# Attention and a low-rank mixer on one core: the first batch's v loaded in two halves, separate places for its heads' probabilities, and the second group's copies on two engines

## The chip, the core and the metric

The kernel runs on one core of one Trainium2 chip. The metric is the device time in microseconds of one execution. The kernel before was run three times (383.29, 383.66 and 385.33 us; the median, 383.66 us, is its time). One more execution was profiled, and every duration in the text comes from that one.

## The reference

Two layers follow each other. The first is causal attention with a bias made of running sums; the second is a low-rank mixer over the sequence and a feed-forward network (FFN) with a ReLU.

```python
B, H, S, D = 8, 8, 576, 64
scores = (q @ k.T) / sqrt(D)                      # per batch and head
cum = cumsum(max(s, 0), axis=-1)
bias = -(cum[:, :, :, None] - cum[:, :, None, :])
scores = where(causal, -1e9, scores + min(bias, 0))
attn = softmax(scores)                            # sum + 1e-9
x = (attn @ v) -> [B, S, H * D = 512]
h = x.T @ U @ V                                   # U: [576, 32], V: [32, 576]
u = x + h.T
out = u + max(u @ w_ch1, 0) @ w_ch2               # w_ch1: [512, 2048], w_ch2: [2048, 512]
```

Inputs and output are float32. The kernel computes in bfloat16 with float32 accumulation.

## The kernel before, in words

**Groups.** The eight batches form five groups: (0,), (1,), (2, 3), (4, 5), (6, 7). A group goes through two parts. The *front* (`front`) is its attention and its mixing (`attention`, then `mix`); the *back* (`ffn`) is its FFN. The front of group g + 1 is woven into the back of group g, so that TensorE always has FFN products between the small steps of the attention. Group 0 has no back to hide in: its front is `first_attention`, which runs by itself at the start.

**The order is the program's.** The kernel is scheduled by hand (`manual_schedule`): each engine executes its instructions in the order in which the Python code emits them, and semaphores are added for the data. `attention`, `mix` and `ffn` are generators that yield the cost, in microseconds, of what they have just emitted. The loop at the end (lines 829 to 847) emits a piece of the back, adds its cost times a ratio to an account `due`, and emits pieces of the front as long as the account is positive:

```python
ratio = FRONT[g + 1] / (BACK[g] - LEAD[g] - LAG[g])
due, live = -LEAD[g] * ratio, True
```

`FRONT` and `BACK` are the summed costs. `LEAD[g]` is how much of the back of group g is emitted before the next front begins; `LAG[g]` is how much is meant to be left when that front has ended.

**How q and k get into place.** TensorE needs q and k with the head dimension on the partitions. For the first two groups, `load_six` loads them by a DMA issued on GpSimd (which also converts to bfloat16) into tiles `six` of 96 partitions, two heads or four at a time, and `turn_six` turns a pair of heads: six TensorE transposes (line 438) into one PSUM bank, then two copies (line 451) out of it, one from partitions 0 to 63 and one from 64 to 127, into the even and odd columns of `kT` or `qT`. Its argument `by` names the engines of the two copies; without it both are on VectorE. For later groups, q and k go through DRAM (`kq_rows`) and DMA transposes on SyncE (`turn_kq`).

**Attention of a head.** `scores` makes the scores of one head in four quanta (lines 459 and 466). Each fills one of three PSUM banks `ps_s`, and ScalarE takes the exponential (line 471) into a tile `p` of probabilities. For the first group masked entries are made very negative by extra products (`bound`, line 466); for later groups VectorE masks `p` (line 631). `weigh` multiplies a head's `p` with v (15 products, line 511, into one of two banks `ps_pv`) and VectorE divides by the row sums (lines 517, 521, 526). The tiles `p` come from a ring of five, `pT`. The last two rows of tiles are read with their ends padded, so `clear` sets the columns behind `P_END` to zero once at the start.

**The first batch.** `first_attention` turns the first two pairs of heads, calls `prepare_second` (which emits GpSimd's loads for the second group and w2), and then goes over the eight heads. Between a head's quanta it places a `stir` (products without use, which keep TensorE active), a turn of a later pair, a `weigh` of an earlier head, or a step of the second group's running sums (`cumulate(1, 2)`). The last pair's k (`turns[6]`) is turned after head 3, its q (`turns[7]`) after head 4. After the loop come the mixing of the first batch (`ux_first`, `turn_first`) and the first three blocks of its FFN (`begin`, line 587).

**GpSimd's queue.** Before the heads GpSimd issues, in this order: k and q of heads 0 to 1, 2 to 3, 4 to 5 (`load_six`, line 203); all of the first batch's v (`load_v(0)`: four transfers of 128 rows, line 229, and a tail of 64 rows, line 235); k and q of heads 6 to 7; the four pieces of w1 (line 247). `prepare_second` continues with U and V, k and q of batch 1, v of batch 1 and the four pieces of w2 (line 253). A transfer issued on GpSimd first waits until the one eight issues before it has landed, because there are eight semaphores for them. SyncE issues the smaller transfers: rows of the running sums, the rows of ones, U, V, s, and the stores.

**Space.** Until the first FFN fills it, the tile `hT` (seen as `flat`, 18432 columns) holds other things: U and V and the rows of ones (`ones`, columns 2048 to 2623), the first batch's `six` (4096 to 10239) and the source of `stir` (10240 to 10367). The FFN's block nf writes columns 1152 nf to 1152 nf + 511 of it at first (line 786).

Of the kernel before, what the change touches and what calls it, by code (L numbers as in the profile page):

```python
# [24 lines left out]
TAIL = 4  # L25
# [6 lines left out]
P_W = P_END + 64  # L32
AUG = 4

A_K, A_Q, A_ONE, A_ALL = slice(0, 4), slice(3, 7), slice(3, 6), 7
# [12 lines left out]
def kernel(  # L48
# [12 lines left out]
    nc = tc.nc  # L61
    B, H, S, D = q.shape
# [6 lines left out]
    BH = B * H  # L69
# [31 lines left out]
    pT = [const([128, P_W], BF16, f"pT{i}") for i in range(5)]  # L101
# [20 lines left out]
    aug = nc.dram_tensor("aug_rows", (A_ALL, BH, S), BF16, kind="Internal").ap()  # L122
# [13 lines left out]
    flat = hT[:, :, :].rearrange("p a c -> p (a c)")  # L136
    stage = flat[:, :2048].bitcast(FP32)
    stirrer = flat[:, 10240:10368]
    ones = flat[:BH, 2048 : 2048 + S]
    n6 = H * SUB * D  # L140
    later = [const([128, H, SUB * D], BF16, f"six{i}") for i in range(2)]
    six = [
# [25 lines left out]
    def load_UV():  # L168
        nc.sync.dma_start(
            out=U_f[:, :4], in_=moe_U[:512].rearrange("(t p) r -> p t r", p=128)  # L170
        )
        nc.sync.dma_start(out=U_f[:64, 4], in_=moe_U[512:576])
        nc.sync.dma_start(out=V_f[:R], in_=moe_V)
        nc.sync.dma_start(out=U_f[64:128, 4], in_=moe_U[512:576])
        nc.sync.dma_start(out=V_f[R : 2 * R], in_=moe_V)
# [24 lines left out]
    def load_six(g, h0, h1):  # L200
        hs = slice(h0, h1)
        for to, src in zip(six[g], (k, q)):
            nc.gpsimd.dma_start(  # L203
                out=to[:, hs, :].rearrange("p h (s d) -> p h s d", d=D),
                in_=src[GROUPS[g][0], hs].rearrange("h (p s) d -> p h s d", s=SUB),
            )
# [15 lines left out]
                    transpose=True,  # L222
                )

    def load_v(g):
        dest = v_raw[g % 2]
        for bi, b in zip(SIDES[g], GROUPS[g]):
            for t in range(4):
                nc.gpsimd.dma_start(  # L229
                    out=dest[:, 5 * bi + t, :, :D],  # L230
                    in_=v[b, :, 128 * t : 128 * t + 128].rearrange("h p d -> p h d"),
                )
        for bi, b in zip(SIDES[g], GROUPS[g]):
            c = 64 * (bi or g == 0)
            nc.gpsimd.dma_start(
                out=dest[c : c + 64, TAIL, :, :D],
                in_=v[b, :, 512:576].rearrange("h p d -> p h d"),
            )

    def load_group(g):  # L240
# [130 lines left out]
    for t in (U_cat, V_cat):  # L371
# [5 lines left out]
        out=before_v, in_=before_v, compare_op=ALU.is_ge, fill=0.0, base=0,  # L377
# [3 lines left out]
        out=before_v, in_=before_v, compare_op=ALU.is_ge, fill=0.0, base=-1,  # L381
# [4 lines left out]
    for _ in cumulate(0, 1):  # L386
# [3 lines left out]
        out=neg[:, 64:], in_=neg[:, 64:], compare_op=ALU.is_ge, fill=NEG, base=0,  # L390
        pattern=[[1, 128]], channel_multiplier=-1,
    )
    for base, c, m in ((64, 1, -1), (-64, 0, 1)):
        nc.gpsimd.affine_select(
            out=neg[:, :64], in_=neg[:, :64], compare_op=ALU.is_ge, fill=NEG, base=base,
            pattern=[[c, 64]], channel_multiplier=m,
        )
    load_v(0)
    load_six(0, 6, 8)
    load_UV()  # L400
    load_s(1, B)
    place_ones(SECOND, (nc.sync, nc.sync))
    for j in range(4):
        load_w1(j)
    nc.sync.dma_start(
        out=aug[A_ONE].rearrange("r n s -> n r s"),
        in_=ones.unsqueeze(1).to_broadcast([BH, 3, S]),
    )
    for t in pT:
        clear(t[:, P_END:])  # L410
    nc.sync.dma_start(
        out=kq[:, :, PAIR:].rearrange("i n c -> (i n) c"), in_=pT[0][: 2 * BH // 2, P_END:]
# [119 lines left out]
    def next_p():  # L532
        n_p[0] += 1
        return pT[(n_p[0] - 1) % len(pT)]

    def first_attention():

        turns = [(hp, which) for hp in range(4) for which in range(2)]
        for i, (hp, which) in enumerate(turns[:4]):
            if i == 1:
                turn_six(0, hp, which, (nc.scalar.copy, nc.scalar.copy))
            else:
                turn_six(0, hp, which)
            stir((3, 14, 6, 46)[i])
        prepare_second()
        done, second = [], cumulate(1, 2)
        for h in range(H):  # L550
            n, hh = h // 2, h % 2
            p = next_p()
            quanta = scores(kT_all, qT_all, p, PW * n + S * hh, 448, True)
            next(quanta)
            next(quanta)
            if h == 7:
                ux_first((0, 1), nc.vector.tensor_copy)

            if h > 4:
                weigh(*done.pop(0))  # L560
            else:
                stir(3)
            next(quanta)
            if h < 4:
                stir(4)
            next(quanta)
            done.append((0, p, 0, h))
            if h in (2, 4, 6):
                next(second)
            if h < 2:  # L570
                turn_six(0, *turns[h + 4])
            elif h == 3:
                turn_six(0, *turns[6])
            elif h == 4:
                turn_six(0, *turns[7], (nc.scalar.copy, nc.vector.tensor_copy))
            if h > 3:
                weigh(*done.pop(0))
        turn_first((0, 1), 0, 256, nc.scalar.copy)
        ux_first((2,), nc.vector.tensor_copy)
        weigh(*done.pop(0))  # L580
        turn_first((0, 1), 256, 512, nc.scalar.copy)
        turn_first((2,), 0, 512, nc.scalar.copy)
        begun = [bank("s", 3) for _ in range(3)]

        def begin(nf, kts, c0, c1):
            for kt in kts:
                nc.tensor.matmul(
                    begun[nf][:, c0:c1], lhsT=w1[:, kt, 128 * nf : 128 * nf + 128],
                    rhs=uT[:, kt, c0:c1], start=(kt == 0 and c0 == 0), stop=False,
                )  # L590

        for nf in range(3):
            begin(nf, (0, 1), 0, 256)
        ux_first((3,), nc.vector.tensor_copy)
        for nf in range(3):
            begin(nf, (0, 1), 256, 512)
        for nf in range(3):
            begin(nf, (2,), 0, 512)
        turn_first((3,), 0, 256, nc.vector.tensor_copy)
        turn_first((3,), 256, 512, nc.scalar.copy)  # L600
        for _ in second:
            pass
        return begun
# [7 lines left out]
    def attention(g, side):  # L611

        pending = None
        turns = [(hp, which) for hp in range(4) for which in range(2)] if g == 1 else []


        for cost in (0.25, 1.8, 0.9) if turns else ():
            turn_six(g, *turns.pop(0))
            yield cost
        for hp in range(H // 2):  # L620
            n = pairs.index((g, hp))
            for hh in range(2):
                for i, bi in enumerate(SIDES[g]):
                    p = next_p()
                    quanta = scores(
                        kT_all, qT_all, p, place(n).start + (2 * i + hh) * S,
                        512 if bi == 0 else 448,
                    )
                    yield next(quanta)
                    yield next(quanta)  # L630
                    nc.vector.tensor_tensor(  # L631
                        p[:, D4:O1], p[:, D4:O1], keep[bi], ALU.min
                    )
                    if turns:
                        turn_six(g, *turns.pop(0))
                        yield 0.25
                    if pending is not None:
                        weigh(*pending)
                        yield 0.48
                    for cost in quanta:  # L640
                        yield cost
                    pending = (g, p, bi, 2 * hp + hh)
                    for _ in range(2):
                        next(side, None)
                    if n > 10 and (hh, i) == (0, 0):
                        bias_rows(n + 1)
            if g == 1 and hp == 1:
                nc.vector.tensor_copy(x_sb[1][:64, TAIL, :], x_sb[0][:64, TAIL, :])


            late = {5: 8, 6: 9, 7: 10, 8: 11}
            if n - 1 in late:
                bias_rows(late[n - 1])
            if n in late:
                turn_kq(late[n])
            if n > 9:
                turn_kq(n + 2)
            if g == 2 and hp == 0:

                for t in (kT(11), qT(11)):  # L660
                    nc.gpsimd.tensor_copy(hold, t[:1, PW : PW + 1])
                load_group(g + 1)
            if g > 2 and hp == 1:

                c = (2 * hp) * D
                nc.gpsimd.tensor_copy(hold, x_sb[g % 2][:1, 0, c : c + 1])  # L666
                load_group(g + 1)
        weigh(*pending)
        yield 0.48
        for _ in side:  # L670
            pass
# [147 lines left out]

    LEAD = [5.0, 11.0, 8.0, 0.0]
    FRONT = [0.0, 17.3, 24.6, 22.3, 22.3]
    BACK = [27.4, 34.3, 61.7, 61.7, 61.7]

    LAG = [0.0, 0.0, 4.5, 4.5]

    begun = first_attention()
    for g in range(len(GROUPS)):
# [48 lines left out]
```

## Time and profile before

| what | value |
|---|---|
| median of three runs | 383.66 us |
| the profiled execution: its time, and the span from its first to its last instruction | 384.49 us, 382.8 us |
| busy share of the span: TensorE, ScalarE, VectorE, GpSimd | 96%, 54%, 42%, 17% |
| mean granted TensorE clock | 0.991 |
| first product of group 0's FFN on the full inner dimension (line 606) | 35.82 us |
| first product with w2 (line 791) | 51.42 us |
| group 1's first FFN product | 84.80 us |
| group 2's first FFN product | 146.84 us |

The names of the engines in the profile are PE (TensorE's products), PEld (its weight loads), ACT (ScalarE), DVE (VectorE), POOL (GpSimd) and SP (SyncE). A line of the timeline gives the start in us, the busy time, the engine, the line of the kernel, the operation, what is written from what, the count, and in brackets how long the engine stood idle before it and what released it. Instructions of one kind that follow each other are merged into one line. A matmul's own duration counts its way through the array, so that consecutive ones overlap.

### The profile page before, as it was taken

To read this page: it belongs to the slowest core of one execution; us is meant where nothing else is said; L and a number is where in the kernel's file an instruction comes from. 1 tells how busy PE (TensorE), PEld (TensorE's weight loads), DVE (VectorE), ACT (ScalarE), POOL (GpSimd) and SP (SyncE) were. 2 spreads that over 40 slices of the span, in tenths; PEclk is the share of its full clock that TensorE was granted. 3 is DMA by queue.
4 is the path that set the end of the run, shared out by engine and by line. 5 is a ranking of instruction groups with operands and counts; after the bars stand their busy time and mean duration, and the time that the engine had idled before them with its cause. 6 is when DMAs were issued, how large, how long until landed. Compare 5 with 4: busy or idle time off the path is not lost.

```text
span 382.8 us, 8201 instructions
## 1 busy us (share of the span) xinstructions
PE 367.0 (96%) x3310; PEld 224.7 (59%) x3310; DVE 158.9 (42%) x373; ACT 205.6 (54%) x459; POOL 65.7 (17%) x104
## 2 busy tenths in 40 slices
PE   7889997989999999999999999999999999999995
PEld 7777554547766645666665446666655445665442
DVE  6555699470346664132344382232244360000221
ACT  4666763408987704989754206888844006773000
POOL 8694642100053200005320000000000000000000
PEclk9989999999999999999999999999999999999999
DMA  7999999998979999954997566840011143000122
GB/s 97 155 210 187 181 215 182 130 137 169 201 132 214 133 154 206 139 114 68 201 158 159 130 160 130 159 98 1 2 57 55 57 107 102 0 3 27 76 63 82
DMA packets 127780, 46.41 MB, mean 121 GB/s; under 512 B 109278, under 2 KB 122846, under 8 KB 127742
## 3 DMA queue, kind: packets, MB, share of 16 engines
q0 software_dynamic: 51376, 18.50, 48.7%
q1 hardware_dynamic: 76182, 27.35, 37.1%
q8 instruction: 26, 0.43, 0.5%
q14 instruction: 12, 0.10, 0.1%
q10 hardware_dynamic: 184, 0.03, 0.1%
HBM read 37.52 MB, written 16.97 MB: 142 GB/s over the span
## 4 chain that ended last, share of the span: by engine, by line
PE 85%; DVE 7%; POOL 2%; DMA 2%; issue 1%; ACT 1%; POOLq 0%; ACTq 0%; DVEq 0%
PE ps_f L606 32%; PE ps_f L791 30%; PE ps_s L459 10%; PE ps_pv L511 8%; DMA hT<-in_k_dram 2%; DVE x_sb L765 2%; PE ps_f L761 1%; PE ps_f L723 1%; POOL v_raw L229 1%; POOL hT L203 1%; DVE qT L451 1%; DVE kT L451 1%; ACT pT L471 1%; DVE o L802 1%; PE ps_pv L747 1%
## 5 line engine op out<-in xcount | busy, mean ns | idle before, releaser
L471 ACT ACTIVATE pT<-ps_s 128x448 bf16<-128x448 f32 (+1 forms) x256 | 119.3, 513 | 68.2 <-PE ps_s L459 66.5
L791 PE MATMUL ps_f<-w,hT 128*128 128x512 bf16 x576 | 148.4, 381 | 0.7 <-DVE x_sb L765 0.6
L606 PE MATMUL ps_f<-uT,w 128*128 128x384 bf16 (+2 forms) x756 | 142.4, 325 | 0.8 <-DVE uT L752 0.8
L786 ACT ACTIVATE hT<-ps_f 128x384 bf16<-128x384 f32 (+2 forms) x189 | 93.9, 497 | 66.6 <-PE ps_f L606 64.0
L606 PEld LDWEIGHTS <-w 128*128 128x128 bf16 x759 | 69.9, 98 | 39.0 <-issue 1.1
L791 PEld LDWEIGHTS <-hT 128*128 128x128 bf16 x576 | 52.2, 98 | 50.0 <-issue 4.3
L459 PE MATMUL ps_s<-qT,kT 68*128 68x128 bf16 (+4 forms) x576 | 79.0, 242 | 0.4 <-ACT pT L471 0.3
L631 DVE TENSOR_TENSOR pT<-pT,keep 128x576 bf16<-128x576 bf16 x56 | 25.6, 457 | 107.9 <-ACT pT L471 107.6
L459 PEld LDWEIGHTS <-kT 68*128 68x128 bf16 x576 | 46.1, 98 | 31.5 <-issue 3.3
L802 DVE TENSOR_TENSOR o<-x_sb,ps_f 128x512 f32<-128x512 bf16 x36 | 24.7, 686 | 78.7 <-PE ps_f L791 75.1
L511 PEld LDWEIGHTS <-pT 128*128 128x128 bf16 x960 | 37.5, 98 | 13.5 <-DVE qT L451 2.6
L511 PE MATMUL ps_pv<-v_raw,pT 128*128 128x65 bf16 x960 | 40.9, 194 | 2.8 <-DVE qT L451 1.9
L229 POOL DMA_DIRECT2D v_raw<-in_v_dram x32 | 28.2, 892 | 29.3 <-PE ps_s L459 12.2
L521 DVE TENSOR_TENSOR x_sb<-ps_pv,rec 128x320 bf16<-128x320 f32 (+1 forms) x64 | 29.3, 458 | 2.2
L765 DVE TENSOR_TENSOR x_sb<-x_sb,ps_f 128x512 bf16<-128x512 bf16 x32 | 20.8, 685 | 5.2 <-PE ps_f L761 5.1
L666 POOL COPY hold<-x_sb 1x1 bf16<-1x1 bf16 x2 | 0.4, 176 | 102.8 <-DVE x_sb L521 102.8
L517 DVE RECIPROCAL rec<-ps_pv 128x5 f32<-128x5 f32 x64 | 12.5, 195 | 6.2 <-PE ps_pv L511 5.4
L166 PE MATMUL ps_pv<-hT 128*128 128x128 bf16 x136 | 11.6, 239 | 1.1 <-DVE hT L132 1.1
L761 PE MATMUL ps_f<-ux_sb,V_cat 128*128 128x512 bf16 x32 | 11.8, 379 | 0.5 <-DVE x_sb L765 0.3
L166 PEld LDWEIGHTS <-hT 128*128 128x128 bf16 x136 | 10.0, 109 | 1.7 <-DVE hT L132 1.1
L526 DVE TENSOR_SCALAR x_sb<-ps_pv,rec 64x64 bf16<-64x64 f32 x32 | 9.3, 291 | 0.5
L451 DVE COPY kT<-ps_f 64x576 bf16<-64x576 bf16 x8 | 6.4, 798 | 5.0 <-PE ps_f L438 5.0
(90 smaller groups left out, 137.4 us busy)
## 6 DMA issues: line engine op xcount, KB each, us to landing
out_dram<-o SPq DMA_DIRECT2D x32, 256.0 KB
v_raw<-in_v_dram POOLq DMA_DIRECT2D x32, 128.0 KB, 14.6
w<-in_moe_w_ch_dram POOLq DMA_DIRECT2D x8, 512.0 KB, 11.7
kq_rows<-in_k_dram POOLq DMA_DIRECT2D x6, 576.0 KB, 10.0
kq_rows<-in_q_dram POOLq DMA_DIRECT2D x6, 576.0 KB, 13.4
out_dram<-o SPq DMA_DIRECT2D x8, 128.0 KB
hT<-in_k_dram POOLq DMA_DIRECT2D x4, 144.0 KB, 4.4
hT<-in_q_dram POOLq DMA_DIRECT2D x4, 144.0 KB, 5.0
```

Source lines behind the costliest of these rows:

```text
L166: nc.tensor.matmul(ps[:, :128], lhsT=stirrer, rhs=stirrer, start=True, stop=True)
L229: nc.gpsimd.dma_start(out=dest[:, 5 * bi + t, :, :D], in_=v[b, :, 128 * t : 128 * t + 128].rearrange("h p d -> p h d"),)
L459: nc.tensor.matmul(ps[:, col : col + n], lhsT=kt_[:KA, c + kc : c + kc + 128], rhs=qt_[:KA, c + qc : c + qc + n], start=start, stop=stop,)
L471: nc.scalar.activation(p[:, at : at + n], ps[:, :n], EXP, scale=scale)
L511: nc.tensor.matmul(pv3[:, it, :], lhsT=p[:, at : at + 128], rhs=vr[:, TAIL if j == 4 else 5 * bi + j, h, :], start=(j == 0), stop=(j == it),)
L521: nc.vector.tensor_mul(x[:, 5 * bi : 5 * bi + n, h * D : h * D + D], pv3[:, :n, :D], rec[:, :n].unsqueeze(2).to_broadcast([128, n, D]),)
L606: nc.tensor.matmul(f1[:, : c1 - c0], lhsT=w1[:, kt, 128 * nf : 128 * nf + 128], rhs=uT[:, kt, c0:c1], start=(kt == 0), stop=(kt == 3),)
L631: nc.vector.tensor_tensor(p[:, D4:O1], p[:, D4:O1], keep[bi], ALU.min)
L765: nc.vector.tensor_add(x[:, t, :], x[:, t, :], hp_)
L786: nc.scalar.activation(hT[:, nf, c0:c1], f1[:, :cw], RELU)
L791: nc.tensor.matmul(f2, lhsT=hT[:, kt, 128 * t : 128 * t + 128], rhs=w2[:, kt, :], start=(kt == 0), stop=(kt == 15 and g > 0),)
L802: nc.vector.tensor_add(o, x_sb[g % 2][:, t, :], f2)
```

## The change

- `load_v` takes a range of heads. The first batch's v is issued as heads 0 to 3 (five transfers of half the size), then k and q of heads 6 and 7, then v of heads 4 to 7 (five more).
- The eight heads of the first batch get a tile of probabilities each (`first_p`: the five of `pT` and three in free columns of `hT`), and all eight are cleared behind `P_END`.
- In `first_attention` the turn of the last k moves from the end of head 3 to its middle (in place of a `stir`), the turn of the last q from the end of head 4 to the end of head 3. The weighings start one head earlier, at the end of head 3; head 7 has one less. Head 4 gets the second `stir`.
- The transfer of the rows of ones to DRAM (`aug[A_ONE]`, on SyncE) moves from the start to the end of head 6.
- In `attention`, all eight turns of the second group are copied by ScalarE (partitions 0 to 63) and VectorE (64 to 127), where VectorE made both copies.
- `LEAD` goes from 5, 11, 8, 0 to 10, 11, 10, 0, and `LAG` from 0, 0, 4.5, 4.5 to 1.5, 1.5, 4.5, 4.5.

```diff
+    first_p = pT + [flat[:, 10368 + P_W * i : 10368 + P_W * i + P_W] for i in range(3)]
...
-    def load_v(g):
+    def load_v(g, h0=0, h1=H):
         dest = v_raw[g % 2]
         for bi, b in zip(SIDES[g], GROUPS[g]):
             for t in range(4):
                 nc.gpsimd.dma_start(
-                    out=dest[:, 5 * bi + t, :, :D],
-                    in_=v[b, :, 128 * t : 128 * t + 128].rearrange("h p d -> p h d"),
+                    out=dest[:, 5 * bi + t, h0:h1, :D],
+                    in_=v[b, h0:h1, 128 * t : 128 * t + 128].rearrange("h p d -> p h d"),
                 )
...
-                out=dest[c : c + 64, TAIL, :, :D],
-                in_=v[b, :, 512:576].rearrange("h p d -> p h d"),
+                out=dest[c : c + 64, TAIL, h0:h1, :D],
+                in_=v[b, h0:h1, 512:576].rearrange("h p d -> p h d"),
...
-    load_v(0)
+    load_v(0, 0, 4)
     load_six(0, 6, 8)
+    load_v(0, 4, 8)
     load_UV()
...
-    nc.sync.dma_start(
-        out=aug[A_ONE].rearrange("r n s -> n r s"),
-        in_=ones.unsqueeze(1).to_broadcast([BH, 3, S]),
-    )
-    for t in pT:
+    for t in first_p:
         clear(t[:, P_END:])
...
-            p = next_p()
+            p = first_p[h]
             quanta = scores(kT_all, qT_all, p, PW * n + S * hh, 448, True)
             next(quanta)
             next(quanta)
-            if h == 7:
+
+            if h == 3:
+                turn_six(0, *turns[6])
+            elif h == 7:
                 ux_first((0, 1), nc.vector.tensor_copy)
-
-            if h > 4:
+            elif h > 4:
                 weigh(*done.pop(0))
             else:
                 stir(3)
             next(quanta)
-            if h < 4:
+            if h < 5:
                 stir(4)
             next(quanta)
             done.append((0, p, 0, h))
             if h in (2, 4, 6):
                 next(second)
+            if h == 6:
+
+                nc.sync.dma_start(
+                    out=aug[A_ONE].rearrange("r n s -> n r s"),
+                    in_=ones.unsqueeze(1).to_broadcast([BH, 3, S]),
+                )
             if h < 2:
                 turn_six(0, *turns[h + 4])
             elif h == 3:
-                turn_six(0, *turns[6])
-            elif h == 4:
                 turn_six(0, *turns[7], (nc.scalar.copy, nc.vector.tensor_copy))
-            if h > 3:
+            if h > 2:
                 weigh(*done.pop(0))
...
+        shared = (nc.scalar.copy, nc.vector.tensor_copy)
         for cost in (0.25, 1.8, 0.9) if turns else ():
-            turn_six(g, *turns.pop(0))
+            turn_six(g, *turns.pop(0), shared)
             yield cost
...
                     if turns:
-                        turn_six(g, *turns.pop(0))
+                        turn_six(g, *turns.pop(0), shared)
                         yield 0.25
...
-    LEAD = [5.0, 11.0, 8.0, 0.0]
+    LEAD = [10.0, 11.0, 10.0, 0.0]
...
-    LAG = [0.0, 0.0, 4.5, 4.5]
+    LAG = [1.5, 1.5, 4.5, 4.5]
```

## The prediction

> **What bounds the kernel now.** First the page's engine row and the clock row (tenths of full speed, 40 slices of 9.57 us):
>
> ```profile
> PE 367.0 (96%) x3310; PEld 224.7 (59%) x3310; DVE 158.9 (42%) x373; ACT 205.6 (54%) x459; POOL 65.7 (17%) x104
> PEclk9989999999999999999999999999999999999999
> ```
>
> TensorE is the bound almost everywhere, so time can only come from stretches where it stands still or runs slow. The table by stretches (columns: PE, PEld, DVE, ACT, POOL busy; clock; DMA) finds them:
>
> ```profile
> 20.00:32.00 12.00, 11.63 (x207) 10.32 (x208) 8.44 (x22) 8.40 (x18) 9.28 (x19) 0.86 1.26 208
> 48.00:56.00 8.00, 7.59 (x90) 4.79 (x89) 7.69 (x20) 5.62 (x14) 3.54 (x4) 1.00 1.22 216
> 56.00:66.00 10.00, 7.95 (x91) 4.37 (x88) 9.54 (x23) 3.98 (x9) 3.36 (x4) 0.97 1.57 190
> 66.00:80.00 14.00, 13.25 (x107) 6.84 (x105) 7.50 (x20) 4.52 (x10) 1.50 (x3) 0.90 1.98 133
> 150.00:215.00 65.00, 64.89 (x642) 41.30 (x640) 21.66 (x58) 47.78 (x109) 11.51 (x15) 1.00 1.07 140
> ```
>
> VectorE is busy 17.2 of 18 us from 48 to 66 while PE idles 2.5 and then sits at clock 0.90; from 150 on nothing is left (0.1 us idle in 65). All that the change can win lies before about 85 us, where the second group's FFN begins (84.80), and a little at the next such border, 147 us. The timelines of PE and POOL show the first hole:
>
> ```profile
> 17.24 0.28 PE L459 MATMUL ps_s<-qT,kT 68*128 68x192 bf16 x2
> 20.37 0.43 PE L438 MATMUL ps_f<-identity,hT 96*128 96x96 bf16 x6 [2.85 <-DMA hT<-in_k_dram]
> 7.35 3.53 POOL L229 DMA_DIRECT2D v_raw<-in_v_dram  x4
> 10.85 0.72 POOL L235 DMA_DIRECT2D v_raw<-in_v_dram  x1
> 11.52 0.69 POOL L203 DMA_DIRECT2D hT<-in_k_dram  x1
> ```
>
> The last pair's k is issued behind all of v, at 11.52, and lands 8.8 us later. PE waits 2.85 us in order, although heads 4 and 5 need none of that data; the granted clock is then 0.63 from 20 to 24.
>
> The second hole is VectorE's: 16 copies of 0.80 us (line 451) for the second group, which PE ends up waiting for:
>
> ```profile
> 64.96 0.51 PEld L511 LDWEIGHTS <-pT 128*128 128x128 bf16 x15 [2.17 <-DVE qT L451]
> ```
>
> One turn in the first batch is already shared between ScalarE and VectorE, and shows how sharing behaves:
>
> ```profile
> 23.30 0.81 ACT L451 COPY qT<-ps_f 64x576 bf16<-64x576 bf16 x1
> 24.14 0.81 DVE L451 COPY qT<-ps_f 64x576 bf16<-64x576 bf16 x1 [1.68 <-ACT qT L451]
> ```
>
> The halves ran one after the other (24.11 end, 24.14 start). Last, the weights. A POOL issue waits for the transfer eight issues earlier, so these give the landings of the four w2 pieces, 45.4, 47.9, 50.5, 53.2:
>
> ```profile
> 45.47 0.73 POOL L193 DMA_DIRECT2D kq_rows<-in_q_dram  x1 [0.82 <-DMA w<-in_moe_w_ch_dram]
> 48.01 0.91 POOL L229 DMA_DIRECT2D v_raw<-in_v_dram  x1 [1.81 <-DMA w<-in_moe_w_ch_dram]
> 50.55 0.88 POOL L229 DMA_DIRECT2D v_raw<-in_v_dram  x1 [1.62 <-DMA w<-in_moe_w_ch_dram]
> 53.26 1.75 POOL L229 DMA_DIRECT2D v_raw<-in_v_dram  x2 [1.83 <-DMA w<-in_moe_w_ch_dram]
> ```
>
> PE first uses w2 at 51.4 and its last piece at 57.0: only 3.8 us of slack.
>
> **The change, part by part.**
>
> **v in halves.** A half tile has as many pieces as today's tail, so 0.72 us an issue; half a tail I put at 0.62 (the step 0.88 to 0.72, continued). Ahead of k: 4 x 0.72 + 0.62 = 3.5 instead of 4.25, so k is issued at 10.8. More counts that 0.29 MB of v and the 0.22 MB of ones (moved too) no longer move before it: at the 155 GB/s of 12 to 20 us that is 3.3 us, k at 16.9. Bounds: 20.2 (nothing gained) and 16.0 (both savings whole). PE reaches the turn at 16.7. POOL issues ten v transfers for five, 6.4 us for 4.25; the added 2.2 us lie in its 3.3 us of waits between the w1 issues, and w1, six and w2 keep their places in a stream that is never empty. The second half must land by head 6, about 22.5; it stands where q stood (landed before 22.5), and is late at worst by about 1 us.
>
> The Trainium skill, "DMA: Bandwidth & Descriptors", Bandwidth, speaks against this: transfers under 64 KB are dominated by descriptors, its fixed cost is about 2.0 us each, and a half tail is 32 KB. By it five more transfers would add up to 10 us if they ran singly; the POOL rows show v issued every 0.88 us with many in flight.
>
> **Own places for probabilities, ones later.** Three more clears of 0.05 us on VectorE at 5.6, under PE's stirring. The places lie in hT's columns of blocks 9 to 13, which the FFN fills some 8 us after the last reader: nothing. The ones' transfer is issued on SyncE after head 6, near 24.5, ahead of three rows that are not needed before 45. Block 2 of hT overwrites its source near 33; it would have to take over 8 us to cost anything (today issued at 12.4, done by 18.4).
>
> **First batch on PE and ScalarE.** Head 3 is done near 17.6 to 18; q's turn and head 0's weighing (0.46) follow, head 4 starts near 19 and takes 2.2 us of PE, so head 5 starts at 21.5 instead of 23.9. Its successors run at full clock (1.85 instead of 2.27 for head 5: 0.4), and one weighing has left head 7 (0.45). The first product moves from 35.82 to **32.5** (bounds 31.9 and 35.8).
>
> **LEAD and LAG of the first FFN.** LEAD 10 for 5 holds the second group's front back; the ratio rises from 0.77 to 1.09. The 13 remaining blocks and 3 last products take 3 x 0.215 + 13 x 0.86 = 11.8 us, and only three turns (0.6) fit between: PE would be at w2 at 44.9, where it is still landing. The second product begins at 45.4 instead of 51.4, and head 0's scores at 45.7, against 45.05 today. So the 3.3 us won in the first batch do not show as an earlier front; they pay for FFN work done before it. w2's later pieces hold PE by up to 0.9 us each; that is mostly under the next term.
>
> **Shared copies.** Weighings 0 to 4 of the second group start at 48.98, 52.68, 56.54, 60.42, 64.97: 3.7 to 4.55 apart, which is VectorE's sum of mask 0.45, copies 1.6, weighing 0.91, cumulative sums about 0.7, o 0.37 = 4.0. After: one copy of 0.80 leaves; the other waits for ScalarE's. If ScalarE is ahead, 0.45 + 0.8 + 0.91 + 0.7 + 0.26 = 3.1; if both start at the end of the second exp, 0.35 more, 3.5. PE itself needs 1.42 + 1.3 = 2.7. I take 3.3, keep 2.7 and 4.0. ScalarE pays 0.8 on top of 1.8 a head, under the period; in the last three FFN blocks its 2.4 us stand before relus, under the wait for w2. Sum: weighing 0 at 45.7 + 3.4 = 49.1; weighing 4 at 49.1 + 4 x 3.3 = 62.3; weighing 7 three PE periods later, 70.5 (today 74.56). From there to the second FFN today 10.2; LAG lets the front's end, 1.0 us of which now runs bare, fall under the FFN: 9.5. The second FFN starts at **80.0**, against 84.8: 4.8 won.
>
> **LAG 1.5 at 147, LEAD 10 at the third FFN.** PE idles 0.7 there and waits on VectorE's sums; I take 0.3 won (0 to 0.7). The later LEAD only moves work within a full PE: 0, plus or minus 0.3.
>
> Sum: 5.1 of the profiled execution's 384.49 (span 382.8 and 1.7 around it) gives 379.4. That execution lies 0.8 above the median 383.66, so on the scale of medians **378.6**. With its terms at their bounds (heads 2.7 to 4.0; product 31.9 to 34.4) 375.5 to 382.
>
> **Rivals.**
>
> Copies side by side. The Trainium skill, "PSUM — Partial Sum Buffer", PSUM bank collisions, lets two engines use one bank at the same time if they are in different quadrants, as these two halves are. The trace's only pair (23.30, 24.14) ran in series. If side by side, every head costs 3.1 and weighing 0 comes 0.4 sooner: 378.6 - 0.8 - 0.4 = 377.4. Chance 0.07.
>
> k is no earlier, because other queues and not v fill the engines: the first product stays at 35.8, head 0 at 48.8, the second FFN 3.1 later at 83.1: 381.7. For it: 20.2 is also when the rate rises from 161 to 211 GB/s. Chance 0.14, half within the bound of no change.
>
> Slower: ScalarE's copy becomes a link of every head's chain. VectorE's queue is in order, so mask, weighing and sums stand behind a copy that stands behind ScalarE's exps. In full series a head is 1.0 exps + 0.8 + 0.8 + 0.91 + 0.7 + 0.45 = 4.7: weighing 0 at 50.4, 4 at 69.2, 7 at 77.4, the FFN at 86.9, 2.1 late: 385.5. It decides from 4.2 a head. For it: VectorE's 1.68 us wait at 22.5. Against: PE has a third score bank and runs ahead, so the exps of the next head need not wait for VectorE. Chance 0.11.
>
> **How the numbers follow.** The likeliest case has 0.62; the remaining 0.06 I spread evenly over faster, the same and slower. Faster by over 0.5% (which is about what a measurement can tell from no change, 1.9 us): 0.62 + 0.07 + 0.07 + 0.02 = 0.78; within: 0.07 + 0.02 = 0.09; slower: 0.13. The range runs from 375.5 to 384.5: it leaves out the slower cases, and little below.
>
> **What would show it.** Right: no wait of PE for k above 1 us near 17, clock 1.0 from 20 to 32, first product near 32.5; short waits (under 1 us) for w2 from 45 to 53; 16 second-group copies split 8 and 8, VectorE's starting as ScalarE's end; weighings 3.1 to 3.5 apart; the second FFN near 80 and everything behind it moved by the same amount. Wrong: PE still stopped for k until 20; a relu waiting for the ones' transfer near 33; weighings 4.2 or more apart with VectorE waiting for ScalarE; v's second half late at head 6; or the transposes for the third group, issued from 62.5 when its rows land, becoming the wait at 92.

## The result and the profile after

The changed kernel takes **381.11 us** (median of six runs, 380.97 to 381.47) against 383.88 us for the kernel before (median of six, 383.29 to 385.71). The ratio is 0.9919, with a 95% interval of 0.9895 to 0.9942: faster by 0.8%. The forecast was 378.6 us with a range of 375.5 to 384.5. The direction held; of the 5.1 us forecast, 2.8 came on the scale of medians. The kernel before is timed in 56 more executions beside the experiments: the 18 with a mean granted clock of 0.998 or more have a median of 382.4 us, the 31 with 0.991 or less one of 384.3. The changed kernel's six ran at 0.998 to 1.000, so that against equal clocks it gains 1.3 us. The profiled execution took 381.14 us with a span of 379.1 (before: 384.49 and 382.8).

The engine row and the clock row of the page after:

```profile
PE 362.7 (96%) x3279; PEld 223.7 (59%) x3311; DVE 152.6 (40%) x368; ACT 211.5 (56%) x467; POOL 68.8 (18%) x109
PEclk9999999999999999999999999999999999999999
```

ScalarE has taken about 6 us from VectorE (eight copies of 0.80). The clock row has no dip any more. The table by stretches after, with the columns as in the prediction:

```profile
20.00:32.00 12.00, 11.49 (x192) 9.63 (x190) 7.64 (x26) 8.10 (x19) 10.30 (x19) 1.00 1.25 210
48.00:56.00 8.00, 6.86 (x84) 4.56 (x84) 6.01 (x17) 5.34 (x12) 3.37 (x4) 1.00 1.22 216
56.00:66.00 10.00, 8.84 (x105) 5.53 (x106) 9.49 (x25) 6.95 (x17) 2.65 (x4) 1.00 1.45 204
66.00:80.00 14.00, 12.61 (x115) 6.84 (x116) 10.36 (x23) 3.39 (x8) 2.23 (x3) 1.00 1.90 145
```

From 48 to 56 PE is now idle for 1.1 us where it was idle for 0.4, and VectorE has air there (6.0 of 8). PE's idle time has changed its cause, as the next lines show. The timelines of POOL and PE at the first hole:

```profile
7.37 3.02 POOL L231 DMA_DIRECT2D v_raw<-in_v_dram  x4
10.35 0.66 POOL L237 DMA_DIRECT2D v_raw<-in_v_dram  x1
10.96 0.69 POOL L205 DMA_DIRECT2D hT<-in_k_dram  x1
16.68 0.42 PE L437 MATMUL ps_f<-identity,hT 96*128 96x96 bf16 x6
```

A half tile costs 0.75 us of issue, a half tail 0.66, and all ten transfers of v 7.4 us; k is issued at 10.96 and PE turns it at 16.68 without a wait. PE's timeline where w2 is first used:

```profile
45.13 0.38 PE L797 MATMUL ps_f<-w,hT 128*128 128x512 bf16 x1 [1.17 <-DMA w<-in_moe_w_ch_dram]
47.60 0.59 PE L797 MATMUL ps_f<-w,hT 128*128 128x512 bf16 x2 [0.76 <-DMA w<-in_moe_w_ch_dram]
50.15 0.59 PE L797 MATMUL ps_f<-w,hT 128*128 128x512 bf16 x2 [0.52 <-DMA w<-in_moe_w_ch_dram]
52.69 0.59 PE L797 MATMUL ps_f<-w,hT 128*128 128x512 bf16 x2 [0.57 <-DMA w<-in_moe_w_ch_dram]
```

Each of the four pieces of w2 holds PE, 3.0 us together. And two turns of the second group, from the timeline of all engines:

```profile
49.97 0.80 ACT L450 COPY kT<-ps_pv 64x576 bf16<-64x576 bf16 x1
50.80 0.81 DVE L450 COPY kT<-ps_pv 64x576 bf16<-64x576 bf16 x1 [0.20 <-ACT kT L450]
53.95 0.80 ACT L450 COPY qT<-ps_pv 64x576 bf16<-64x576 bf16 x1
54.79 0.80 DVE L450 COPY qT<-ps_pv 64x576 bf16<-64x576 bf16 x1 [0.24 <-ACT qT L450]
```

The halves run one after the other in all eight turns. In six, VectorE starts 0.03 to 0.08 us after ScalarE's end; in the last two (ScalarE from 57.06 and 59.88) it comes 0.7 and 1.9 us later, because its own queue keeps it. Once the scores have begun (45.60), VectorE waits for ScalarE by 0.24 us at most. Each VectorE copy waits for a semaphore that ScalarE's copy raises, so the order is the program's; whether the two engines could read the bank side by side was not tried.

### The profile page after: what moved, and what is told of

It is laid out like the page before. It is cut to its first block, busy times and chain, and to the rows that moved or that the text cites. A ratio compares the mean times of both kernels' runs of the same rounds, so it can differ in the third digit from the quotient of the medians.

```text
span 379.1 us, 8156 instructions
## 1 busy us (share of the span) xinstructions
PE 362.7 (96%) x3279; PEld 223.7 (59%) x3311; DVE 152.6 (40%) x368; ACT 211.5 (56%) x467; POOL 68.8 (18%) x109
## 4 chain that ended last, share of the span: by engine, by line
PE 77%; DMA 9%; DVE 5%; POOL 4%; issue 2%; ACT 2%; POOLq 0%; ACTq 0%
PE ps_f L797 29%; PE ps_f L611 28%; PE ps_s L458 9%; PE ps_pv L510 6%; DMA six<-in_q_dram 4%; DMA w<-in_moe_w_ch_dram 3%; PE ps_f L767 2%; DMA v_raw<-in_v_dram 2%; DVE x_sb L771 2%; ACT pT L470 2%; PE ps_f L729 1%; POOL hT L205 1%; DVE o L808 1%; PE ps_pv L753 1%; POOL v_raw L231 1%
## 5 line engine op out<-in xcount | busy, mean ns | idle before, releaser
L797 PE MATMUL ps_f<-w,hT 128*128 128x512 bf16 x546 | 142.3, 379 | 4.5 <-DMA w<-in_moe_w_ch_dram 3.0
L470 ACT ACTIVATE pT<-ps_s 128x448 bf16<-128x448 f32 x244 | 113.5, 513 | 58.5 <-PE ps_s L458 55.7
L611 PE MATMUL ps_f<-uT,w 128*128 128x384 bf16 (+2 forms) x755 | 140.2, 325 | 0.1
L510 PEld LDWEIGHTS <-pT 128*128 128x128 bf16 x915 | 35.9, 97 | 10.3 <-ACT pT L470 0.7
L510 PE MATMUL ps_pv<-v_raw,pT 128*128 128x65 bf16 x915 | 39.1, 194 | 1.3 <-DVE qT L450 0.8
L231 POOL DMA_DIRECT2D v_raw<-in_v_dram x36 | 30.8, 863 | 30.3 <-PE ps_s L458 10.9
L450 DVE COPY kT<-ps_pv 64x576 bf16<-64x576 bf16 x4 | 3.2, 805 | 11.5 <-ACT kT L450 11.5
```

The costliest lines, as they stand in the source:

```text
L231: nc.gpsimd.dma_start(out=dest[:, 5 * bi + t, h0:h1, :D], in_=v[b, h0:h1, 128 * t : 128 * t + 128].rearrange("h p d -> p h d"),)
L470: nc.scalar.activation(p[:, at : at + n], ps[:, :n], EXP, scale=scale)
L510: nc.tensor.matmul(pv3[:, it, :], lhsT=p[:, at : at + 128], rhs=vr[:, TAIL if j == 4 else 5 * bi + j, h, :], start=(j == 0), stop=(j == it),)
L611: nc.tensor.matmul(f1[:, : c1 - c0], lhsT=w1[:, kt, 128 * nf : 128 * nf + 128], rhs=uT[:, kt, c0:c1], start=(kt == 0), stop=(kt == 3),)
L797: nc.tensor.matmul(f2, lhsT=hT[:, kt, 128 * t : 128 * t + 128], rhs=w2[:, kt, :], start=(kt == 0), stop=(kt == 15 and g > 0),)
```

## The experiments

Marks read from the traces, in us. "First product" is that of group 0's FFN (31.16 in the changed kernel), "w2" PE's waits for it in sum, "weighings" the mean distance between weighings 0 to 4 of the second group, then the starts of group 1's and group 2's FFN and the distance between the two. "Time" is the median of the runs.

| kernel | first product | w2 | weighing 0 | weighings | FFN 1 | FFN 2 | FFN 1 to 2 | time |
|---|---|---|---|---|---|---|---|---|
| before | 35.82 | 0 | 48.96 | 4.00 | 84.80 | 146.84 | 62.04 | 383.88 |
| changed | 31.16 | 3.02 | 50.58 | 3.21 | 80.03 | 143.03 | 63.00 | 381.11 |
| 1: LAG[1] 0 | 31.56 | 2.98 | 50.96 | 3.21 | 80.40 | 142.45 | 62.05 | 380.34 |
| 2: LEAD[0] 5 | 31.36 | 0.28 | 44.28 | 3.23 | 75.10 | 138.11 | 63.01 | 377.10 |
| 3: copies on VectorE | 31.40 | 2.51 | 51.71 | 3.96 | 84.17 | 147.17 | 63.00 | 384.32 |
| 4: v whole | 36.38 | 0 | 53.04 | 3.24 | 82.59 | 145.60 | 63.01 | 383.27 |
| 5: first batch only | 31.64 | 0 | 44.98 | 4.02 | 80.89 | 142.93 | 62.04 | 380.38 |
| 6: shared copies only | 34.93 | 0 | 48.78 | 3.41 | 80.66 | 142.98 | 62.32 | 380.49 |
| 7: ring of five | 32.02 | 1.79 | 51.22 | 3.22 | 80.71 | 144.00 | 63.29 | 381.36 |
| 8: LEAD[0] 5, LAG[1] 0 | 31.55 | 0.47 | 44.47 | 3.27 | 75.48 | 137.53 | 62.05 | 376.19 |
| 9: no wait for w2 | 32.32 | 0 | 48.97 | 3.12 | 78.06 | 141.07 | 63.01 | 380.33 |
| 10: LEAD[0] 3, LAG[1] 0 | 31.40 | 0 | 44.20 | 3.18 | 75.82 | 137.87 | 62.05 | 377.00 |
| 11: VectorE copies first | 31.55 | 2.14 | 51.08 | 3.72 | 82.58 | 145.58 | 63.00 | 384.00 |

All but the last column stand for one execution each; the medians of the kernel before beside the experiments were 383.67 (1 to 4), 383.35 (5 to 8) and 383.93 (9 to 11). In experiment 7 a wait of 0.96 us before the first product with w2 is put down to a relu and is not in its 1.79.

**1. LAG[1] back at 0.**

```diff
-    LAG = [1.5, 1.5, 4.5, 4.5]
+    LAG = [1.5, 0.0, 4.5, 4.5]
```

> The changed kernel with LAG[1] back at 0. Theory (the tighter weaving costs): from group 1's first FFN product to group 2's the changed kernel takes 63.00 us (80.03 to 143.03), the kernel before 62.04 (84.80 to 146.84). With LAG[1] = 0 the stretch is 62.0 to 62.2 again and the time about 380.2 us. Rival (the 1.0 us comes from something else that moved with the change, transposes or loads that are now nearer to their use): the stretch stays at 63.0 and the time at 381.1.

Measured: 62.05 between the two FFNs, 380.34 us (379.88 to 380.69). The theory holds to the hundredth: in every one of the kernels with 1.5 the stretch is 63.0 or more, in every one with 0 it is 62.04 to 62.32. Where it is lost, the tables of the two stretches (heads, then mixing of group 2) show, before first, then changed:

```profile
96.20:134.95 38.75, 38.27 (x486) 26.24 (x483) 20.55 (x58) 31.37 (x77) 11.69 (x16) 1.00 1.21 169
134.95:146.84 11.89, 11.19 (x79) 5.72 (x79) 9.62 (x17) 0.00 (x0) 0.00 (x0) 1.00 1.58 162
```

```profile
91.44:129.61 38.17, 37.24 (x475) 25.90 (x479) 19.94 (x57) 31.77 (x77) 10.39 (x15) 1.00 1.10 168
129.61:143.03 13.42, 12.36 (x84) 6.31 (x86) 11.02 (x19) 0.00 (x0) 1.32 (x2) 1.00 1.91 154
```

With less FFN work between the heads PE is idle for 0.93 us in them instead of 0.48, and the work that was held back for the mixing does not fill its waits either: 1.06 idle instead of 0.70.

**2. LEAD[0] back at 5.**

```diff
-    LEAD = [10.0, 11.0, 10.0, 0.0]
+    LEAD = [5.0, 11.0, 10.0, 0.0]
```

> The changed kernel with LEAD[0] back at 5, so that the second group's front begins about 5 us earlier, while w2 is still on its way. Theory (PE's 3.0 us of waits for w2 are lost because the front starts too late to fill them): the waits for w2 fall below 0.5 us in sum, weighing 0 of the second group starts near 44 to 45 instead of 50.6, weighings stay about 3.3 apart, group 1's FFN begins near 77 instead of 80.0 and the time is about 378.3 us. Rival (the front cannot go earlier: the second group's q, landed at 39.8, and its v hold it): weighing 0 not before 48, the time 380.5 to 381.5. Rival (VectorE's and ScalarE's copies disturb the relus of the first product): slower than 381.5.

Measured: 377.10 us (376.22 to 378.05), ratio to the kernel before 0.9845 (0.9807 to 0.9883). The first theory holds in direction and more: group 1's FFN comes 4.9 us earlier than in the changed kernel. PE's waits for w2, in the views of waits of the changed kernel and of this one (total, times, longest):

```profile
PE ps_f L797 <- DMA w<-in_moe_w_ch_dram: 3.0, 4, 1.2
```

```profile
PE ps_f L797 <- DMA w<-in_moe_w_ch_dram: 0.3, 1, 0.3
```

So LEAD 10, part of the change, costs 4 us against LEAD 5 with the rest of the change in place. Experiment 9 asks by which way.

**3. Both copies on VectorE.**

```diff
-        shared = (nc.scalar.copy, nc.vector.tensor_copy)
+        shared = (nc.vector.tensor_copy, nc.vector.tensor_copy)
```

> The changed kernel with both copies of the second group's turns on VectorE again. Theory (VectorE paces the heads with turns): weighings 0 to 4 of the second group are 3.7 to 4.0 apart instead of 3.2, group 1's FFN begins near 83 and the time is about 384 us. Rival (halves that run one after the other win nothing): 381.1, weighings unchanged.

Measured: 384.32 us, weighings 3.96 apart, group 1's FFN at 84.17. The theory holds: sharing is worth 3.2 us here although the halves never overlap. That VectorE has half the copies to do is not the whole reason, as experiment 11 shows. Without sharing, LEAD 10 and the LAGs eat all that the first batch wins: this kernel is not faster than the one before (ratio 1.0019, 0.9996 to 1.0043).

**4. All of v ahead of the last k again.**

```diff
-    load_v(0, 0, 4)
+    load_v(0)
     load_six(0, 6, 8)
-    load_v(0, 4, 8)
```

> The changed kernel with all of v issued before the last pair's k and q again. PE waits for k in the middle of head 3, by 2 to 3.5 us. Theory (w2 takes the place of k: what the first batch wins is given back as waits for w2): the first product moves from 31.16 to about 34, the waits for w2 shrink from 3.0 to about 0.5 us, group 1's FFN begins 0.5 to 1 us later, and the time is about 381.8 us. Rival (the first batch's time goes straight to the end): 383.5 to 384.5.

Measured: 383.27 us, first product at 36.38, group 1's FFN at 82.59. PE's timeline has the wait of before again, and the clock row its dip:

```profile
20.32 0.43 PE L436 MATMUL ps_f<-identity,hT 96*128 96x96 bf16 x6 [2.75 <-DMA hT<-in_k_dram]
```

```profile
PEclk9989999999999999999999999999999999999999
```

The time is nearer to the rival's lower number (383.5) than to the theory's (381.8), but the way there is the theory's: of 5.2 us lost at the first product, 2.6 arrive at group 1's FFN and 2.2 in the time, as w2's waits fall from 3.0 to 0. The loss of the first batch was put too small. Head 0's scores start 0.7 us later than in the changed kernel (12.03 against 11.31); the other 4.5 are the wait of 2.75 and the slow clock after it (0.81, 0.50 and 0.84 in the three stretches of 2 us from 20 to 26, about 1.7 us). It also shows that the order of the issues, and not the moved transfer of ones, is what brings k early.

**5 and 6. Each half of the change alone**, in the kernel before. Experiment 5 is the changed kernel with these lines back as they were:

```diff
-    LEAD = [10.0, 11.0, 10.0, 0.0]
-    LAG = [1.5, 1.5, 4.5, 4.5]
-        shared = (nc.scalar.copy, nc.vector.tensor_copy)
+    LEAD = [5.0, 11.0, 8.0, 0.0]
+    LAG = [0.0, 0.0, 4.5, 4.5]
+        shared = (nc.vector.tensor_copy, nc.vector.tensor_copy)
```

> Of the change only the first batch's part (v in halves, eight places, the order of turns and weighings, the later ones); LEAD, LAG and the second group's copies as before. Theory (the first batch's time reaches the end if the front isn't held back for it): the first product at 31.2 as in the changed kernel, the front begins 4.6 us earlier than before and VectorE paces it as before (weighings 3.7 to 4.0 apart), waits for w2 under 0.5 us, group 1's FFN near 80.5 and the time near 379.5 us. Rival (w2's landing takes the place of k whatever LEAD is): waits for w2 of 2 us or more, group 1's FFN at 82.5 or later and the time above 381.5.

Measured: 380.38 us (ratio 0.9906, 0.9868 to 0.9943), no wait for w2, group 1's FFN at 80.89. The theory holds, with the time 0.9 us above its number. Experiment 6 is the kernel before with

```diff
-            turn_six(g, *turns.pop(0))
+            turn_six(g, *turns.pop(0), (nc.scalar.copy, nc.vector.tensor_copy))
```

at both places in `attention`.

> The kernel before with only the second group's copies shared. Theory (VectorE paces the heads with turns): weighings 0 to 4 of the second group 3.2 to 3.4 apart instead of 3.7 to 4.5, group 1's FFN near 81.8 instead of 84.8 and the time near 380.8 us (before 383.7). Rival (sharing only pays where LEAD 10 has put the front later): weighings 3.6 apart or more, the time above 382.5.

Measured: 380.49 us (ratio 0.9915, 0.9884 to 0.9946), weighings 3.41 apart, group 1's FFN at 80.66. The theory holds; 0.9 us of it lie in a first product that came earlier in this execution, in which PE waited for k by 1.65 us and not 2.85. Each half alone brings as much as the whole change.

**7. The first batch's probabilities in the ring of five.**

```diff
-            p = first_p[h]
+            p = next_p()
...
-    for t in first_p:
+    for t in pT:
```

> The changed kernel with the first batch's probabilities in the ring of five again (head 5 writes where head 0's lay). Theory (the places hide nothing: head 0 is weighed at 17.7, 3 us before head 5's first exp): times and stretches as in the changed kernel, first product at 31.2, 380.8 to 381.4 us. Rival (the places are what lets the heads run on): the first product 0.5 us later or more, and the time with it.

Measured: 381.36 us (380.82 to 382.25). The first product came at 32.02, which the rival wanted; but PE's timelines, of the changed kernel and of this one, show that head 0 was late already. First head 0's scores, then the first product:

```profile
11.31 0.36 PE L458 MATMUL ps_s<-qT,kT 68*128 68x64 bf16 x4
...
31.16 0.81 PE L611 MATMUL ps_s<-uT,w 128*128 128x512 bf16 x3 [0.46 <-DVE rest L339]
```

```profile
12.18 0.36 PE L458 MATMUL ps_s<-qT,kT 68*128 68x64 bf16 x4 [0.19 <-DMA hT<-in_moe_V_dram]
...
32.02 0.81 PE L611 MATMUL ps_s<-uT,w 128*128 128x512 bf16 x3 [0.46 <-DVE rest L339]
```

19.85 us from the one to the other in the first, 19.84 in the second: the separate places bring nothing and cost nothing.

**8. LEAD[0] 5 and LAG[1] 0 together** (experiments 1 and 2 in one).

> The changed kernel with LEAD[0] = 5 and LAG[1] = 0 together. Both theories so far (the front started too late for the waits for w2; the tighter weaving of the next front costs 1.0 us): group 1's FFN near 75.1, group 2's 62.0 us later, near 137.1, the time near 376.2 us. Rival (the two overlap, and one covers the other): 377.0 or more.

Measured: 376.19 us (375.20 to 377.06), ratio to the kernel before 0.9799 (0.9768 to 0.9830), as forecast. This is the best version found, 4.9 us below the changed kernel's median.

**9. Batch 0's second product without w2.** It reads w1's columns, which have long landed; batch 0's output is therefore another.

```diff
-                    f2, lhsT=hT[:, kt, 128 * t : 128 * t + 128], rhs=w2[:, kt, :],
+                    f2, lhsT=hT[:, kt, 128 * t : 128 * t + 128],
+                    rhs=w2[:, kt, :] if g else w1[:, kt % 4, 512 * (kt // 4) : 512 * (kt // 4) + 512],
```

> The changed kernel, except that batch 0's second product reads w1's columns in place of w2 (that batch's FFN output is then another; shapes, order and all transfers are the same), so that it never waits for w2. Theory A (the 3.0 us of waits for w2 are what the changed kernel lost against its variant with LEAD[0] = 5): the waits for w2 before 55 us are gone, group 1's FFN begins near 77 and the time is near 378.2. Theory B (the second group's front sets the end: it takes 38 to 40 us from its first turn, whatever PE waits for beside it, and LEAD 10 starts it 5 us later): the time of the waits comes back as waits for VectorE and ScalarE, group 1's FFN at 79 to 80 and the time 380.2 to 381.1.

Measured: group 1's FFN at 78.06, 380.33 us (379.18 to 381.10). The stretch from the first product to group 1's FFN, in the tables of the changed kernel, of this one and of experiment 2:

```profile
31.16:80.03 48.87, 43.11 (x389) 24.25 (x396) 29.16 (x69) 28.41 (x56) 17.86 (x24) 1.00 1.65 182
```

```profile
32.32:78.06 45.74, 42.53 (x388) 24.15 (x395) 29.05 (x69) 28.03 (x56) 17.09 (x23) 1.00 1.61 185
```

```profile
31.36:75.10 43.74, 41.97 (x388) 24.27 (x395) 29.63 (x69) 27.77 (x56) 18.20 (x24) 1.00 1.60 185
```

Of the 5.1 us by which LEAD 5 shortens the stretch, 3.1 go with the waits for w2 (theory A), and 2.0 need LEAD 5 itself, as theory B has it; LEAD 5 also lowers the ratio of the weaving, from 1.09 to 0.83, which was not tried apart from the earlier start. PE's idle part falls from 5.8 to 3.2 to 1.8. In the time only 0.8 of the 3.1 arrive. In the profiled execution 1.2 are a later first product, and the remaining 2.0 arrive (379.18 against 381.14). Five of the other six executions had a mean granted clock of 0.994 to 0.998 and took 380.24 to 381.10; the sixth, at 1.000, took 379.63. A lower clock thus goes with a part of what is missing in the median; why it fell stays open, since these executions have no trace.

**10. LEAD[0] 3.**

```diff
-    LEAD = [10.0, 11.0, 10.0, 0.0]
+    LEAD = [3.0, 11.0, 10.0, 0.0]
```

and LAG[1] 0.

> The changed kernel with LEAD[0] = 3 and LAG[1] = 0. Theory B (the front's start sets the end): the first turn of the second group comes 2 us earlier than with LEAD 5; its q and k have landed by then (33.2 and 34.6), so weighing 0 is near 42.5 and group 1's FFN near 73.8, the time near 374.6 us. Rival (with LEAD 5 the start is early enough; v, or the rows of sums, or PE's own work hold it): group 1's FFN at 75.0 or later, the time 376 to 377.

Measured: weighing 0 at 44.20, where LEAD 5 had it; group 1's FFN at 75.82; 377.00 us (376.07 to 381.35). Theory B fails below 5: an earlier start brings nothing more. The first turn comes 1.9 us earlier than in experiment 8 (34.20 against 36.08), head 0's scores 0.9 (39.88 against 40.74), its weighing 0.3. LEAD 3 also lowers the ratio from 0.83 to 0.76, so that more FFN work lies between the steps of the front; whether this or a wait takes the lead back was not tried.

**11. VectorE copies first.**

```diff
-        shared = (nc.scalar.copy, nc.vector.tensor_copy)
+        shared = (nc.vector.tensor_copy, nc.scalar.copy)
```

> The changed kernel with the engines of the two copies exchanged: VectorE copies partitions 0 to 63, ScalarE then 64 to 127. Theory (the second copy waits for the first whichever it is; ScalarE's exps then stand behind VectorE's queue): weighings 0 to 4 are 3.4 to 4.0 apart instead of 3.2, ScalarE waits for VectorE in most turns, group 1's FFN at 81.5 or later, time 382 to 384. Rival (the halves run side by side where the engines are both free, and the order is of no account): 380.8 to 381.4, and copies of one turn that overlap in time.

Measured: 384.00 us, weighings 3.72 apart, group 1's FFN at 82.58. The theory holds. A turn in the timeline:

```profile
55.56 0.80 DVE L450 COPY qT<-ps_pv 64x576 bf16<-64x576 bf16 x1
56.39 0.80 ACT L450 COPY qT<-ps_pv 64x576 bf16<-64x576 bf16 x1 [1.36 <-DVE qT L450]
```

ScalarE stands for 1.36 us behind the busier engine's copy, with the next exps behind it. The order of the two names is worth 2.9 us. VectorE has half the copies to do here too, and yet only 0.3 us are left of the 3.2 that sharing won.

## Why the prediction was right, and where it was not

**The first hole.** Right: PE no longer waits for k, the clock stays at 1.00. The first product came at 31.16, beyond the early bound of 31.9 (32.5 was forecast); k was in time at 16.68 without the short wait that was allowed for. Head 4 began at 18.19 and not near 19, head 5 at 20.13 and not at 21.5, and from there on the stretch is as forecast. Experiment 4 puts the price of the hole at 4.5 us. It also makes the case of the rival in which k is no earlier: group 1's FFN came at 82.59, against that rival's 83.1; of the 1.6 us between its time of 383.27 us and the rival's 381.7, 1.25 are the LAG term below.

**LEAD and w2.** The step said that what the first batch wins does not show as an earlier front and that w2 is still landing at 45. Right: second product at 45.13 (45.4), head 0's scores at 45.60 (45.7). The waits for w2, 0.5 to 1.2 each where up to 0.9 was allowed, were sized well but put "mostly under the next term": that failed. Weighing 0 came at 50.58 instead of 49.1, and experiment 9 shows that the waits lengthen the stretch in full. The step stopped one question short: whether LEAD 5 would be better with the rest of the change (it is, by 4 us).

**Shared copies.** Right: in series, weighings 3.21 apart (3.3). The rival of copies side by side did not come about, in any of the eight turns, because a semaphore orders the halves. The rival of ScalarE as a link of the chain did not come about, but experiment 11 shows its mechanism with the engines exchanged, at 0.5 us a head. Weighing 7 begins with one product and pauses before the others. From its second product, the mark that the prediction took (74.56 before, 70.24 now), the last three heads took 6.8 us instead of the 8.2 forecast, and from there to group 1's FFN it took 9.8, not 9.5 (10.24 before, 9.79 now): LAG[0] brought at most 0.45 of its 0.7. With the late weighing 0 these cancel, so that 80.03 against 80.0 is better than its terms.

**LAG at 147.** Wrong in sign: 0.3 won was forecast, 0.96 lost was measured (62.04 to 63.00), and experiment 1 gives it back alone. The term looked at the border's idle 0.7 and not at the heads that pay for it. In the time it is worth 0.8 (experiment 1) and 0.9 (experiment 8 against 2). From group 2's FFN to the end of the span little changed (235.9 and 236.1), as forecast for LEAD[2].

**From 378.6 to 381.11.** 1.25 us are the LAG term. 0.35 lie around the span (1.69 before, 2.04 after). About 0.8 is the scale: the forecast took the profiled execution's distance above the median (0.8) along, but after, the profiled execution lies on the median (381.14).

**Sums that do not come out.** Ten issues of v at the prediction's own prices (0.72 and 0.62) are 7.0 us, not 6.4; measured were 7.4, 3.1 more than before and not 2.2. That did no harm, since w2's pieces landed no later. The upper end of 382 us takes the first product at 34.4, which is derived nowhere; with heads of 4.0 us it would give 383.3, still inside the range.

## What to carry to other kernels

When a stall is removed, look up what lands next: here the time won ran into the next load in the queue, and a later start of the next front, which left PE to wait for that load, cost 4.0 us, more than either half of the change won alone. Test the parts of a tuned bundle alone and without its retuned constants; each half was worth as much as the whole, and with two constants set back the whole was worth more than twice a half (7.2 us against 3.0 and 2.9). When a copy is split between two engines that take turns, try both orders; here it paid to let the less loaded one go first.

## What the runs showed of the hardware

The granted clock fell to 0.50 in a stretch of 2 us after single waits of PE of 1.65 (experiment 6, 22 to 24), 1.92 and 2.85 (the kernel before), 1.99 (experiment 5) and 2.75 us (experiment 4), and to 0.53 after one of 2.04 (experiment 3). It did not fall after one of 1.74 in experiment 3 (1.00 from 66 to 80), nor after several short ones: 3.0 us of waits in four pieces of at most 1.17 left it at 1.00 (48 to 56 in the changed kernel). So the length of a wait alone did not decide. PE's timelines of experiments 6 and 3:

```profile
19.48 0.43 PE L438 MATMUL ps_f<-identity,hT 96*128 96x96 bf16 x6 [1.65 <-DMA hT<-in_k_dram]
...
67.54 0.62 PE L510 MATMUL ps_pv<-v_raw,pT 128*128 128x65 bf16 x15 [1.74 <-DVE qT L450]
```

and the stretch of experiment 5 in which the wait of 1.99 us lies:

```profile
56.00:66.00 10.00, 7.83 (x70) 4.33 (x70) 7.52 (x19) 3.65 (x8) 2.62 (x3) 0.83 1.53 196
```

The first product's time moved between 31.16 and 32.32 in kernels with the same beginning, most of it with the landing of the second pair's q before 10 us: in the changed kernel and in experiments 1, 2, 5 and 9 the first product follows the turn of that q by 22.87 or 22.88 us, while the turn itself moves from 8.29 to 9.44, where PE waits 1.11 us for that q. The waits for w2 do not swallow such a delay: in experiment 1 the first product came 0.40 us later than in the changed kernel, the waits for w2 were the same (2.98 against 3.02), and group 1's FFN came 0.37 later. The changed kernel's six runs lie within 0.5 us, experiment 2's within 1.8 and the kernel before's within 2.4. Experiment 2's ran at granted clocks of 0.998 to 1.000, so that its spread stays unexplained.
